# q turned by VectorE, attention in 32-row tiles: batches 1 to 7 of a linear-attention and expert kernel

## The chip, the cores and the metric

The kernel runs on one core of a Trainium2 chip. The time is that of the device for one execution, in microseconds (us). Five engines work side by side, each through its own list of instructions: TensorE (PE; its weight loads are listed as PEld), VectorE (DVE), ScalarE (ACT), GpSimd (POOL) and SyncE (SP), which starts most transfers. They wait for each other through semaphores. TensorE writes to PSUM[...]; ScalarE and VectorE carry results from there to SBUF.

## What is computed

The reference is linear attention, followed by a weighted sum of four experts. All is float32.

```python
# q, k, v: (8, 8, 576, 64) = batch, head, token, dimension
kv = np.einsum('bhsd,bhse->bhde', k, v)
out = np.einsum('bhsd,bhde->bhse', q, kv)
rms = np.sqrt(np.mean(out * out, axis=-1, keepdims=True) + 1e-06)
attn = out / rms * g_norm
# (B, H, S, D) -> (B*S, H*D): x is 4608 x 512
x = np.ascontiguousarray(attn.transpose(0, 2, 1, 3)).reshape(B * S, H * D)
p = domain_probs / (domain_probs.sum(-1, keepdims=True) + 1e-09)
for e in range(4):                       # w1: 4 x 512 x 1024, w2: 4 x 1024 x 512
    h = np.maximum(x @ w1[e], 0.0)
    out += p[:, e:e + 1] * (h @ w2[e])
```

## The kernel before

The work is cut into nine chunks of 512 tokens: the first 512 tokens of each of the eight batches, and a ninth that gathers the 64 left tokens of all batches. For each of four experts it goes through the nine chunks, with an up projection (`up`) and a down projection (`down`, `down_deep`). Both replace a product of 2x2 blocks by seven products of sums of blocks, most of them at two levels, so TensorE sees long rows of small products. They all go through one helper, which is why so much of the profile has line 356:

```python
    def halves_of(out_, lhsT, rhs, **kw):          # L352 to L356
        for half in range(2):
            cols = slice(half * D, (half + 1) * D)
            nc.tensor.matmul(out_[cols], lhsT=lhsT[:, cols], rhs=rhs, **kw)
```

Nothing is issued in the order of the source. Each operation is entered in a plan with a key (its place in the work), its buffers and a booked cost; `Plan.layout` then fixes the order of every engine before the launch. An engine takes the first operation that is ready within a reach beyond its oldest open one (`REACH`). PSUM banks come in four kinds of two banks each: u1 and u2 for the up products, db for the down products, ab for attention and others.

During the first expert, the attention of batch c + 1 runs inside the stage of chunk c. For batches 1 to 7 it works on pairs of heads (4 pairs), and on two groups of two pairs. Its steps, with the lines that the profile shows:

```python
        # 1. turn q (L693): per pair, four 128x128 transposes to one bank, a ScalarE copy to SBUF
                def turn(eng, bank=bank, qt=qt):
                    for r in range(NR):
                        rs = slice(r * P, (r + 1) * P)
                        if b:
                            nc.tensor.transpose(bank.ap[:, rs], qt.ap[:, rs], ident[:])
                            continue
                ...
        # 2. k.T @ v (L716) of the two pairs of a group, one bank, two 64-column halves (r: the head)
            def key_values(eng, bank=kbank, held=held):
                for o, (kt, vt) in enumerate(held):
                    sets = list(zip(kv_rows(kt), kv_rows(vt)))
                    for j, (ks, vs) in enumerate(sets):
                        for r in range(2):
                            nc.tensor.matmul(
                                bank.ap[r * D:(r + 1) * D, o * D:(o + 1) * D],
                                lhsT=ks[r], rhs=vs[r], start=(j == 0),
                                stop=(j == len(sets) - 1), skip_group_check=True,
                            )
        # 3. attend (L743): q @ kv in 64x64 tiles; head r contracts over its 64 rows, into bank raw[r]
            def attend(eng, raw=raw, kv=kv, pairs=pairs):
                for o, hp in enumerate(pairs):
                    for i in range(NR):
                        for c in range(2):
                            for r in range(2):
                                half = slice(r * D, (r + 1) * D)
                                at = i * P + c * D
                                nc.tensor.matmul(
                                    raw[r].ap[c * D:(c + 1) * D, (o * NR + i) * D:(o * NR + i + 1) * D],
                                    lhsT=qTs[hp].ap[half, at:at + D],
                                    rhs=kv.ap[half, o * D:(o + 1) * D],
                                )
        # 4. scaled(): squares (ScalarE, from PSUM), sums (VectorE), power (GpSimd),
        #    times 1/rms (VectorE, from PSUM) into x
        # 5. turn x (L761): per pair four transposes, then ScalarE copies with the gain
                def turn_x(eng, bank=bank, x=x, o=o):
                    for r in range(NR):
                        rs = slice(r * P, (r + 1) * P)
                        nc.tensor.transpose(
                            bank.ap[:, rs], x.ap[:, o * NT + r * P:o * NT + (r + 1) * P], ident[:])

        # 6. the 64 left tokens: turn q (L787), attend (L805), scale, turn x (L821), store to x_left
        def turn_rem(eng):
            for hp in range(NPAIR):
                nc.tensor.transpose(
                    tb.ap[:, hp * REM:(hp + 1) * REM], qr.ap[0:REM, hp * P:(hp + 1) * P],
                    ident[:REM, :REM],
                )
        ...
        def attend_rem(eng):
            for hp in range(NPAIR):
                for r in range(2):
                    half = slice(r * D, (r + 1) * D)
                    kv, o = kvs[hp]
                    nc.tensor.matmul(
                        rawr[r].ap[0:REM, hp * D:(hp + 1) * D],
                        lhsT=qTr.ap[half, hp * REM:(hp + 1) * REM],
                        rhs=kv.ap[half, o * D:(o + 1) * D],
                    )
        ...
        def turn_xrem(eng):
            for cc in range(NPAIR):
                nc.tensor.transpose(
                    xb.ap[:, cc * REM:(cc + 1) * REM], xr.ap[0:REM, cc * P:(cc + 1) * P],
                    ident[:REM, :REM],
                )
```

q is loaded for each head as `q[b, head, 0:512].rearrange("(p r) d -> p r d", r=4)` to columns that alternate between the two heads of a pair, in runs of 64 elements. The row order of x within a chunk, and so of the output, follows from this: partition p, block r is token 4p + r.

Batch 0 runs ahead of everything, with 128x512 up products (`up_plain`) in its wake; it has its own forms of steps 1 and 2.

## Time and profile before

| | before |
|---|---|
| time, median of three executions | 1688.22 us (1687.34 to 1689.27) |
| span of the profiled execution | 1685.7 us |
| instructions | 66495 |
| granted TensorE clock | 1.00 |
| DMA | 234.27 MB in 172330 packets, 61576 of them under 512 B |
| of attention, from 31 to 350 us: L693 / L716 / L743 / L761 | 100 / 480 / 768 / 96 records on PE |

In the page and the timeline, a row names the line, engine, operation, and output <- input by the names of the buffers with their numbers left out. A TensorE form like 128*64 is rows x columns of the tile of the array that is in use, followed by the moving operand's shape. A float32 matmul call leaves two records, a transpose one. Rows of a timeline give start, modelled length, engine, line, form and count; PE's lengths overlap, so the difference of two starts says more. Some of PE's records can be missing.

### The profile page before, as it was taken

The page shows a single profiled execution, that of the slowest core. Times are in us where ns is not written, and L with a number is a line of the kernel's source. Part 1 is how long each engine was busy: PE and PEld are TensorE (multiplying, and loading weights), DVE is VectorE, ACT ScalarE, POOL GpSimd, SP SyncE. Part 2 cuts the span into 40 slices and gives each one's busy share as a digit, 9 for nine tenths or more (in the row PEclk, how much of TensorE's full clock was granted, in tenths as well). Part 3 has the DMA queues.
Part 4 walks back from the last instruction along what each step waited for, and adds up shares of the span by engine and source line. Part 5 has one row for each costly group of instructions (what it writes and reads, how often), then busy time and mean ns, then how long its engine had stood idle before and what let it go on. Part 6 is the DMA issues. An engine that isn't in the chain of part 4 may idle for free.

```text
span 1685.7 us, 66495 instructions
## 1 busy us (share of the span) xinstructions
PE 1677.6 (100%) x29038; PEld 1572.0 (93%) x29038; DVE 1239.6 (74%) x2045; ACT 975.4 (58%) x2405; POOL 714.9 (42%) x672
## 2 busy tenths in 40 slices
PE   9999999999999999999999999999999999999998
PEld 6687888888889999999999999999999999999996
DVE  4865665575787788777787787877787886877774
ACT  3454555455455666566666566666666666666662
POOL 3613333333444344334455445444446446444431
PEclk9999999999999999999999999999999999999999
DMA  9955553642566344444568444445478444444442
GB/s 236 265 180 151 166 158 101 200 148 94 199 154 166 112 115 115 115 115 114 129 179 198 115 115 115 115 115 114 111 188 200 122 114 115 115 115 115 115 102 51
DMA packets 172330, 234.27 MB, mean 139 GB/s; under 512 B 61576, under 2 KB 112648, under 8 KB 172040
## 3 DMA queue, kind: packets, MB, share of 16 engines
q1 hardware_dynamic: 148968, 193.32, 36.7%
q0 software_dynamic: 23072, 36.71, 15.1%
q8 instruction: 228, 3.74, 0.9%
q14 instruction: 62, 0.51, 0.1%
HBM read 155.79 MB, written 74.19 MB: 136 GB/s over the span
## 4 chain that ended last, share of the span: by engine, by line
PE 98%; DMA 1%; SPq 0%; issue 0%; ACT 0%; DVE 0%
PE u L356 47%; PE db L356 32%; PE ab L356 14%; PE ab L716 1%; PE ab L761 1%; PE ab L693 1%; DMA small<-in_q_dram 1%; PE ab L743 1%; DMA xf<-x 0%; PE ab L805 0%; PE ab L787 0%; PE db L743 0%; PE ab L821 0%; PE ab L1440 0%; SPq L385 0%
## 5 line engine op out<-in xcount | busy, mean ns | idle before, releaser
L379 DVE TENSOR_TENSOR big<-big,big 128x1024 f32<-128x1024 f32 (+1 forms) x517 | 502.0, 985 | 43.3 <-ACT big L959 16.7
L356 PE MATMUL u<-xf,big 128*64 128x128 f32 x7072 | 505.0, 273 | 0.6 <-DMA xf<-x 0.6
L356 PEld LDWEIGHTS u<-xf,big 128*64 128x64 f32 x7072 | 409.4, 137 | 5.2 <-issue 0.9
L356 PE MATMUL u<-xf,w1y 128*64 128x128 f32 x5304 | 382.8, 273 | 0.0
L356 PE MATMUL db<-big,big 128*64 128x128 f32 (+1 forms) x4328 | 362.0, 307 | 0.0
L1003 DVE TENSOR_TENSOR big<-u,snap 128x256 f32<-128x256 f32 x464 | 194.0, 420 | 214.4 <-PE u L356 149.2
L356 PEld LDWEIGHTS u<-xf,w1y 128*64 128x64 f32 x5304 | 307.6, 137 | 4.5 <-issue 1.3
L356 PEld LDWEIGHTS db<-big,big 128*64 128x64 f32 x4328 | 264.4, 137 | 39.3 <-issue 0.5
L995 ACT ACTIVATE snap<-u 128x256 f32<-128x256 f32 x490 | 187.0, 382 | 194.5 <-PE u L356 140.6
L379 POOL TENSOR_TENSOR big<-big,big 128x256 f32<-128x256 f32 (+1 forms) x156 | 192.0, 1234 | 168.9 <-DVE big L379 75.0
L995 ACT ACTIVATE big<-u 128x256 f32<-128x256 f32 x464 | 176.7, 383 | 89.7 <-PE u L356 69.3
L379 POOL TENSOR_TENSOR big<-big 128x512 f32<-128x512 f32 (+1 forms) x76 | 95.3, 1255 | 161.4 <-DVE big L379 104.4
L1304 ACT ACTIVATE snap<-db 128x256 f32<-128x256 f32 (+1 forms) x230 | 82.1, 357 | 114.7 <-PE db L356 102.4
L959 ACT ACTIVATE big<-big 128x1024 f32<-128x1024 f32 x133 | 139.8, 1051 | 4.7 <-DVE big L379 4.3
L1161 POOL DMA_DIRECT2D out_dram<-big x98 | 88.4, 1025 | 56.0 <-ACT big L1138 43.6
L1312 DVE TENSOR_TENSOR big<-ab,snap 128x256 f32<-128x256 f32 x164 | 69.0, 421 | 58.2 <-PE ab L356 28.4
L1342 POOL TENSOR_TENSOR big<-big 128x512 f32<-128x512 f32 x34 | 44.0, 1296 | 154.1 <-DVE big L379 140.8
L995 ACT ACTIVATE u<-u 128x256 f32<-128x256 f32 x245 | 91.0, 372 | 28.6 <-PE u L356 14.1
L379 DVE TENSOR_TENSOR big<-big 128x512 f32<-128x512 f32 (+1 forms) x121 | 103.1, 855 | 0.5 <-ACT big L1138 0.2
L356 PE MATMUL ab<-big,big 128*64 128x128 f32 (+1 forms) x1352 | 94.7, 277 | 0.1
L356 PE MATMUL db<-small,big 128*64 128x128 f32 x1240 | 90.6, 273 | 0.0
L356 PE MATMUL ab<-kv,big 128*64 128x128 f32 x1200 | 83.2, 273 | 0.0
(178 smaller groups left out, 2412.4 us busy)
## 6 DMA issues: line engine op xcount, KB each, us to landing
xf<-x SPq DMA_DIRECT2D x108, 512.0 KB, 3.7
out_dram<-big POOLq DMA_DIRECT2D x82, 256.0 KB, 5.6
xf<-x_h SPq DMA_DIRECT2D x81, 256.0 KB, 3.5
xf<-x SPq DMA_DIRECT2D x81, 256.0 KB, 3.9
x<-xf SPq DMA_DIRECT2D x36, 512.0 KB, 4.9
big<-in_moe_w_dram SPq DMA_DIRECT2D x31, 512.0 KB, 5.2
x_h<-big SPq DMA_DIRECT2D x18, 512.0 KB, 3.4
big<-in_moe_w_dram POOLq DMA_DIRECT2D x17, 512.0 KB, 7.5
```

What stands on the lines that cost most here:

```text
L356: nc.tensor.matmul(out_[cols], lhsT=lhsT[:, cols], rhs=rhs, **kw)
L379: lambda eng: adder(eng).tensor_tensor(out=out_(), in0=a(), in1=b(), op=op),
L693: nc.tensor.transpose(bank.ap[:, rs], qt.ap[:, rs], ident[:])
L716: nc.tensor.matmul(bank.ap[r * D:(r + 1) * D, o * D:(o + 1) * D], lhsT=ks[r], rhs=vs[r], start=(j == 0), stop=(j == len(sets) - 1), skip_g ...
L743: nc.tensor.matmul(raw[r].ap[c * D:(c + 1) * D, (o * NR + i) * D:(o * NR + i + 1) * D], lhsT=qTs[hp].ap[half, at:at + D], rhs=kv.ap[half, ...
L959: lambda eng: nc.scalar.activation(out=b.ap[:], in_=b.ap[:], func=ACT.Relu),
L995: lambda eng: nc.scalar.activation(out=where(), in_=ps.ap[:, 0:HN], func=ACT.Copy),
L1003: lambda eng: nc.vector.tensor_tensor(out=block(whole, a, t), in0=src.ap[:, 0:HN], in1=add_.ap[:], op=ALU.add),
L1161: nc.gpsimd.dma_start(out=dst, in_=cell(i)[parts, :], accum_op=ALU.add)
L1304: lambda eng: nc.scalar.activation(out=where(), in_=group_of(ps.ap), func=ACT.Copy),
L1312: lambda eng: nc.vector.tensor_tensor(out=cell(tq, dq), in0=group_of(src.ap), in1=group_of(add_.ap), op=ALU.add,),
L1342: lambda eng: adder(eng).tensor_tensor(out=whole(to), in0=whole(a), in1=whole(b), op=ALU.add),
```

## The change

For batches 1 to 7 the change replaces `attention` (what it was stays as `opening`, for batch 0 alone).

- q: each group of four heads has one buffer of 128 x 1152, head a on partitions 32a to 32a + 31, sixteen tokens on each partition in runs of 4 KB, the left tokens behind them. VectorE turns it in place in 32x32 blocks, taking even and odd dimensions apart (`dh`). TensorE's turns of q and ScalarE's copies of them go.
- key-values: k is taken by the same parity, so each product has 32 columns; head a fills partitions 32a on.
- attend: the contraction runs over 32 rows, in tiles of 32 rows x 64 columns, one bank for each of four heads (two of kind ab, two of kind db), the two parities accumulated. The left tokens are a fifth block of the same group, so their own turn and attend go.
- the banks are copied to SBUF over the q buffer by VectorE or ScalarE, and the scaling works there.
- x turns: two pairs (eight transposes) in one operation; two 128x128 transposes for the left tokens.
- what follows from it: another order of the rows in output and probabilities for chunks 1 to 7, three small buffers in place of eight, and rules in the planner: operations marked `gang` may keep banks from others that would open them (`opens`), TensorE's reach goes from 0.7 to 1.1, and some down products get an order.

The core of the diff, with cuts marked:

```diff
-    REACH = {"PE": 0.7, "DVE": 0.9, "ACT": 0.9, "POOL": 0.9, "SP": 1.0}
+    REACH = {"PE": 1.1, "DVE": 0.9, "ACT": 0.9, "POOL": 0.9, "SP": 1.0}
...
+                        if op.gang and all(d.start is not None and d.end < t for d in op.deps):
+                            kept.update((b.kind, True) for b in op.outs if b.kind in BANKED)
...
+            plan.add(
+                when - 0.1, dve(QW),
+                lambda eng, qt=qt: nc.vector.transpose(out=by_parity(qt), in_=by_parity(qt)),
+                reads=[qt], writes=[qt],
+            )
...
+            def key_values(eng, bank=kbank, held=held):
+                sets = [list(zip(rows_of(kt), rows_of(vt))) for kt, vt in held]
+                last_ = len(sets[0]) - 1
+                for j in range(last_ + 1):
+                    for dh in range(2):
+                        for a in range(G):
+                            ks, vs = sets[a // 2][j]
+                            nc.tensor.matmul(
+                                bank.ap[a * R:(a + 1) * R, dh * D:(dh + 1) * D],
+                                lhsT=ks[a % 2][:, dh::2], rhs=vs[a % 2],
+                                start=(j == dh == 0), stop=(j == last_), skip_group_check=True,
+                            )
...
+            raw = [Buf(("ab", "ab", "db", "db")[a], f"raw{n}_{a}") for a in range(G)]
+
+            def attend(eng, raw=raw, kv=kv, qt=qt, s=s):
+                for t in range(NR + 1):
+                    for dh in range(2):
+                        for c in range(2) if t < NR else (s,):
+                            at_ = (2 * t + c) * P if t < NR else 2 * NT
+                            for a in range(G):
+                                rs = slice(a * R, (a + 1) * R)
+                                nc.tensor.matmul(
+                                    raw[a].ap[c * D:(c + 1) * D, t * D:(t + 1) * D],
+                                    lhsT=qt.ap[rs, at_ + dh:at_ + P:2],
+                                    rhs=kv.ap[rs, dh * D:(dh + 1) * D],
+                                    start=(dh == 0), stop=(dh == 1), skip_group_check=True,
+                                )
...
+            for a in range(G):
+                evacuate(
+                    when, raw[a],
+                    lambda a=a, raw=raw: raw[a].ap[:, 0:NR * D].rearrange("p (t e) -> p t e", e=D),
...
+            def turn_x(eng, turned=turned, qt=qt):
+                for o in range(2):
+                    for r in range(NR):
+                        nc.tensor.transpose(
+                            turned[o].ap[:, r * P:(r + 1) * P],
+                            qt.ap[:, o * NT + r * P:o * NT + (r + 1) * P], ident[:])
...
+        def turn_left(eng):
+            for o in range(2):
+                nc.tensor.transpose(
+                    xb.ap[:, o * P:(o + 1) * P], xr.ap[:, o * P:(o + 1) * P], ident[:])
...
+                return [(slice(0, P), whole.rearrange(
+                    "(p r a) d -> r a p d", r=NR, a=NR)[i])]
...
-                op.marks = ps, HN
+                    after=(second[-1:] if m in (1, 5) else []) + firsts[t:t + 1],
+                )
+                op.marks, op.opens = (ps, HN), m == 1
...
-                    after=(inner_last[-2:-1] or primed) if mm == 1 else seeds if mm == 5 else (),
+                    after=(inner_last[-2:-1] or primed) + (second[-1:] if mixed else []) if mm == 1 else seeds if mm == 5 else (),
```

## The prediction

> **What bounds the kernel now.** I read the page's first part, then the list of who waited for whom on TensorE, then the table by stretches of time, and last the timeline of TensorE. The first part says that PE has work nearly the whole span, while VectorE and ScalarE have slack:

> ```profile
> PE 1677.6 (100%) x29038; PEld 1572.0 (93%) x29038; DVE 1239.6 (74%) x2045; ACT 975.4 (58%) x2405; POOL 714.9 (42%) x672
> ```

> A busy PE alone could be a PE that is held up inside its pipeline. So the second view: everything that PE ever waited for, in the whole span.

> ```profile
> PE ab L1440 <- POOL ident masks.py:199: 1.4, 1, 1.4
> PE ab L697 <- DMA small<-in_q_dram: 1.0, 2, 0.6
> PE u L356 <- DMA xf<-x: 0.6, 1, 0.6
> PE ab L821 <- ACT big L769: 0.3, 1, 0.3
> ```

> 3.3 us in all, nearly all of it in the first 20 us. Time can come only from PE work that disappears. The third view shows what the other engines have to spare where attention runs. Columns: stretch, length, then busy us and (count) of PE, PEld, DVE, ACT, POOL, the granted clock, DMA share and GB/s.

> ```profile
> 31.00:75.00 44.00, 43.54 (x568) 23.63 (x566) 38.34 (x73) 19.31 (x47) 23.57 (x23) 1.00 0.93 246
> 75.00:120.00 45.00, 45.00 (x663) 36.10 (x659) 29.75 (x56) 24.05 (x56) 13.03 (x16) 1.00 0.66 211
> 120.00:180.00 60.00, 60.00 (x938) 48.79 (x938) 35.46 (x62) 30.05 (x70) 19.63 (x21) 1.00 0.47 138
> 180.00:240.00 60.00, 60.00 (x994) 50.73 (x990) 38.22 (x65) 32.29 (x75) 23.02 (x18) 1.00 0.50 149
> ```

> PE is full. From 120 us VectorE is busy 0.59 to 0.64 of the time, ScalarE 0.50 to 0.54. Only before 75 us is DMA near its limit.

> The fourth view gives the price of each piece of attention on PE. The printed length of a group is a modelled end; I use the difference between one start and the next.

> ```profile
> 86.33 0.61 PE L356 MATMUL u<-xf,big 128*64 128x128 f32 x8
> 86.76 0.61 PE L356 MATMUL u<-xf,w1y 128*64 128x128 f32 x8
> 87.30 0.66 PE L693 MATMUL ab<-ident,small 128*128 128x128 f32 x4
> 87.89 0.66 PE L356 MATMUL u<-xf,big 128*64 128x128 f32 x8
> 88.37 1.34 PE L716 MATMUL ab<-kv 120*64 120x64 f32 x40
> 89.54 1.04 PE L356 MATMUL u<-xf,big 128*64 128x128 f32 x16
> 90.52 0.46 PE L787 MATMUL ab<-ident,small 64*128 64x64 f32 x4
> 90.91 1.09 PE L356 MATMUL u<-xf,w1y 128*64 128x128 f32 x16
> ...
> 92.37 1.16 PE L743 MATMUL ab<-kv,small 64*64 64x64 f32 x64
> 93.46 0.66 PE L356 MATMUL u<-xf,w1y 128*64 128x128 f32 x8
> ...
> 103.16 0.68 PE L805 MATMUL ab<-kv,small 64*64 64x64 f32 x16
> 103.77 0.66 PE L356 MATMUL u<-small,big 128*64 128x128 f32 x8
> ```

> A group of eight 128*64 products between its like takes 0.43 us (86.33 to 86.76). Ahead of a group of another tile shape it takes 0.54 (86.76 to 87.30), after one 0.48 (87.89 to 88.37). Over all attention groups after 31 us I found medians of 0.10 and 0.05 us extra, so each **island** of attention in the stream of 128*64 products costs 0.16 us beside its own length.

> [...] The trace agrees for four tiles: 64 records of the 64*64 attend in 1.09 us are 17 ns apiece, while the median record lasts 218 ns. No run here yet shows eight. [...]

> **The change part by part, on PE, per batch (1 to 7).** Each Python matmul in float32 is two records here (32 calls, 64 records in L743), but a transpose is one.

> I count in **rounds**: calls divided by the tiles that work side by side. Attend: 32 calls on 4 tiles, 8 rounds, 1.09 us: 0.136 per round. Key-values: 20 calls on 2 column tiles, 10 rounds, 1.17: 0.117. Left tokens: 8 calls of which only two row tiles are at work, 4 rounds, 0.61: 0.152. The same price of some 0.12 to 0.15 us holds for all three, which is why I trust it for the new shapes.

> Before: q turns 4 x 0.585 = 2.34; turn of the left q 0.39; key-values 2 x 1.21 (mean of all its groups) = 2.42; attend 2 x 1.09 = 2.18; left attend 0.61; x turns 4 x 0.57 = 2.28; turn of the left x 0.41. Sum 10.6. As a check, all attention groups after 31 us add up to 75.6 us from start to start; 1.4 of these belong to batch 0, and 74.2 / 7 = 10.6. Islands: 80 in that stretch, 3 of batch 0, so 11 per batch, 11 x 0.16 = 1.75. Together **12.35 us per batch**.

> After:
> - the q turns, the turn of the left q and the left attend are gone: VectorE turns q, and the left tokens ride in the main attend.
> - key-values: 40 calls on 4 column tiles, 10 rounds as before: 2 x 1.21 = 2.42. It gains nothing; it makes the parity layout.
> - attend: per group 64 calls on 8 tiles are 8 rounds; the 8 calls for the left tokens use one column half, so 4 tiles, 2 rounds. 10 rounds x 0.136 = 1.36; twice, 2.72.
> - x turns: two pairs in one go, 8 transposes. The trace has eight in a row (83.20 to 84.23, four of x and four of q): 1.03. Twice, 2.06.
> - left x: 2 full transposes in place of 4 small ones, about 0.3 (half of 0.585).
> - islands: 2 + 2 + 2 + 1 = 7, x 0.16 = 1.1.

> Sum 8.6. Saved: 12.35 - 8.6 = 3.75 per batch, and 7 batches give **26 us**. The rest of PE's work (the nested seven-product up and down projections, 360 to 1686 us and most of what is before) keeps its instructions.

> **Beside PE.** Per batch the change takes from ScalarE the four q copies (0.6 each) and the left one (0.4), and adds, for whichever of VectorE and ScalarE is free, eight evacuations of 128x256 (0.38 to 0.42 by the rows of that shape) and eight small ones (I estimate 0.2), some 4.9 us; VectorE gets two turns of 1152 elements, which I estimate at 1.35 us each from the reduction of 1024 elements (1.215 us). Squares, reductions and the scaling stay about as long, but read SBUF. Net some 4 to 5 us per batch on two engines which in a stage of about 60 us have 20 to 30 us each to spare. That is hidden as a sum. The loads of q become 4 KB runs in place of 256 B runs, which can only relieve DMA in the first 75 us. The other output row order, four copies in the normalising of the probabilities and the scheduler's new rules are not PE work.

> **Rivals.** *A: the gang of four banks makes PE wait.* Attend needs both ab and both db banks at once; down products use db. Meanwhile only the up products are left, on u1 and u2, and these need a ScalarE or VectorE copy every 0.44 us. For it: the list of waits has ACT and DVE releasing banks just in time (L995 and L1003 lead their own lists because they wait for PE, so they run close behind it). Against it: the longer reach of PE's list and the rule that keeps banks closed to new openers are there to fill this time. 14 gangs x 0.3 us = 4 us is my allowance; at 1.5 us per gang the gain falls to some 5 us, time 1683. *B: issue bounds the eight tiles.* Should a record never follow another in under 17 ns, attend is 144 x 17 = 2.45 us instead of 1.36, key-values 80 x 17 = 1.36; loss 1.24 x 14 = 17 us, time 1679 (without A's allowance). For it: 17 ns is the closest the trace shows. Against: the price per round is the same at 2 tiles (29 ns a record) and at 4 (17 ns), so nothing has begun to saturate. *C: VectorE becomes the limit in the attention stages.* Its 0.6 share would rise to perhaps 0.67; I give that little weight, except before 75 us where it is at 0.87 and DMA at 0.93; there up to 3 us of batch 1's gain may be lost. *D: the work order improves by the new rules alone.* With 3.3 us of waits there is nothing to win.

> **Range and chances.** 1688.2 - 26 = 1662; plus 4 for A = 1666, and I take off nothing for D: **1666 us**. B with A's allowance is 1683, at the upper end; if the rounds are as short as key-values' 0.117 and no gang waits, attend is 0.19 us less on each of 14 groups, 2.7 us, and the x turns may be hidden next to each other with fewer islands: 1656. So 1655 to 1684. Faster by over 2% means under 1654.5: it would take a saving of 34 us where all of attention on PE is 86; 0.07. Slower by over 2% (above 1722) needs stalls of 60 us; 0.04. Within 2%: 0.89.

> **What would show it.** Right: the q turns gone from PE's groups for batches 1 to 7; attend groups of 144 records lasting 1.3 to 1.45 us from start to start; key-values of 80 records at about 1.2; PE's list of waits still under some 8 us; PE busy down by about 25 us with the rest of PE's groups unchanged in count. Wrong by A: waits of PE on u banks for DVE or ACT in the attention stages. Wrong by B: attend groups above 2 us. Wrong in total if PE's time outside attention changes, for example if the new order of projections makes more changes of tile shape.

## The result: 1.6% slower

The changed kernel takes **1715.85 us** (1710.64 to 1717.48), the kernel before 1688.43 beside it: ratio 1.0158, 95% interval 1.0135 to 1.018. The prediction was 1666 with a range of 1655 to 1684. It is outside, and the sign is wrong. That the time stayed within 2% of the old one, which the prediction gave 0.89, came true by luck: it was meant for a gain.

The first part of the page after:

```profile
PE 1674.4 (98%) x30452; PEld 1577.1 (92%) x30452; DVE 1268.0 (74%) x2065; ACT 973.2 (57%) x2419; POOL 762.8 (45%) x719
```

PE is busy 3 us less than before, not 26 less, and the span is 1713.6 us, so PE now stands idle for 39.2 us; before it was 8.1 (1685.7 - 1677.6). The list of who waited for whom on PE, longest first (us in total, times, longest), says for what:

```profile
PE u L371 <- DVE big L1236: 14.7, 9, 3.8
PE u L371 <- issue: 7.4, 4, 2.7
PE u L371 <- ACT u L1228: 2.7, 2, 2.2
...
PE ab L977 <- issue: 1.5, 2, 1.0
```

Two kinds of wait lead it. One is for VectorE's read of an up-product bank (L1236; a u bank comes free when it is read). The other is "issue": PE waits for nothing that the profile shows. The table by stretches (columns as in the prediction) says where. The changed kernel first, then the kernel before in a stretch far behind the attention:

```profile
75.00:120.00 45.00, 40.29 (x848) 33.54 (x846) 32.63 (x64) 22.14 (x57) 24.65 (x28) 1.00 0.75 236
120.00:180.00 60.00, 56.68 (x1146) 48.06 (x1144) 40.29 (x67) 29.21 (x69) 24.99 (x23) 0.97 0.50 160
...
700.00:1050.00 350.00, 344.67 (x6276) 343.86 (x6273) 267.12 (x428) 215.66 (x542) 162.60 (x149) 1.00 0.54 132
```

```profile
700.00:1050.00 350.00, 349.97 (x6408) 349.43 (x6406) 273.65 (x442) 219.69 (x552) 166.00 (x153) 1.00 0.54 133
```

From 700 to 1050 us no attention runs, only projections with the same instructions. Before, PE is idle for 0.03 us there; after, for 5.3, and 132 records fewer get done. So most of the loss is not where the change was thought to act. From 410 us to the end (the same table, summed) PE is idle for 24.4 us, before for 4.6; from 31 to 410 us it is 11.0 against 0.5. These are two losses with two causes.

**What VectorE waits for.** The timeline of all engines around one of the long waits (start, length, engine, line, what; in brackets the idle time before it and what ended it), cut to the chain:

```profile
469.95 1.90 PE L371 MATMUL db<-big,big 128*64 128x256 f32 x16
472.01 1.23 DVE L394 TENSOR_TENSOR big<-big,big 128x1024 f32<-128x1024 f32 x1 [4.92 <-DMA out_dram<-big]
473.16 0.42 DVE L1236 TENSOR_TENSOR big<-u,snap 128x256 f32<-128x256 f32 x1
...
473.63 0.55 PE L371 MATMUL u<-xf,w1y 128*64 128x128 f32 x6 [1.78 <-DVE big L1236]
```

Read it upwards. PE resumes when VectorE has read the u bank (L1236). VectorE stood still for 4.92 us until a transfer to the output had landed, because its next sum (L394) writes the buffer that this transfer was reading. So the chain is: an output lands late, its buffer comes free late, VectorE is late, PE waits. In the view of the output tensor, the waits of VectorE for it (us in total, times) are 40 us in the changed kernel:

```profile
DVE big L1236: 23.4, 8
DVE big L394: 16.7, 5
```

and 2 us in the kernel before:

```profile
DVE big L1003: 2.0, 2
```

The queues and the time from issue to landing are in the view of the DMA (queue: packets, MB, share; issues: KB each, median us to landing). Before:

```profile
q0 software_dynamic: 23072, 36.71, 15.1%
...
out_dram<-big POOLq DMA_DIRECT2D x82, 256.0 KB, 5.6
```

After:

```profile
q0 software_dynamic: 55328, 36.97, 15.8%
...
out_dram<-big POOLq DMA_DIRECT2D x92, 256.0 KB, 10.8
```

An accumulating transfer of 256 KB now lands after 10.8 us instead of 5.6. The planner books the buffer for 8 us. The queue carries 32,256 packets more: 84 transfers x 384, of 8 bytes each by the trace's records (0.26 MB in all).

**A wait can cost twice.** The granted clock of the whole span is 0.993, before 1.00. Around a wait at 866.95 to 870.75 us the table by stretches reads:

```profile
866.68:870.75 4.07, 0.28 (x6) 0.03 (x1) 1.61 (x3) 0.00 (x0) 0.21 (x1) 1.00 0.51 120
871.70:875.10 3.40, 3.40 (x38) 3.40 (x36) 3.40 (x3) 2.10 (x4) 3.10 (x3) 0.51 0.44 154
876.00:880.00 4.00, 4.00 (x78) 4.00 (x75) 3.25 (x5) 1.92 (x6) 1.71 (x2) 1.00 0.90 130
```

Soon after the wait PE works 3.4 us at half clock: 38 records in 3.40 us, and later 78 in 4.00 at full clock. There are six such windows of 3.41 us, and PE is busy in nearly all of them, so they cost about 6 x 1.7 = 10 us. In the kernel before there is none.

### The profile page after: what moved, and what is told of

The parts are those of the page before. It is cut to its first block, busy times and chain, and to the rows that moved or that the text cites. A ratio compares the mean times of both kernels' runs of the same rounds, so it can differ in the third digit from the quotient of the medians.

```text
span 1713.6 us, 69433 instructions
## 1 busy us (share of the span) xinstructions
PE 1674.4 (98%) x30452; PEld 1577.1 (92%) x30452; DVE 1268.0 (74%) x2065; ACT 973.2 (57%) x2419; POOL 762.8 (45%) x719
## 3 DMA queue, kind: packets, MB, share of 16 engines
q0 software_dynamic: 55328, 36.97, 15.8%
## 4 chain that ended last, share of the span: by engine, by line
PE 89%; DMA 7%; DVE 2%; issue 1%; POOL 1%; ACT 0%; SPq 0%; DVEq 0%; POOLq 0%; ACTq 0%
PE u L371 43%; PE db L371 28%; PE ab L371 13%; DMA out_dram<-big 5%; PE ab L977 1%; DVE big L394 1%; DMA xf<-x 1%; PE ab L1003 1%; PE ab L1035 1%; PE db L1003 1%; PE ab L1678 1%; DMA kv<-in_v_dram 0%; DVE big L1236 0%; POOL big L1580 0%; PE ab L712 0%
## 5 line engine op out<-in xcount | busy, mean ns | idle before, releaser
L394 DVE TENSOR_TENSOR big<-big,big 128x1024 f32<-128x1024 f32 (+1 forms) x505 | 493.4, 993 | 52.1 <-DMA out_dram<-big 16.7
L371 PE MATMUL u<-xf,big 128*64 128x128 f32 x7072 | 520.5, 274 | 4.5 <-issue 2.6
L371 PEld LDWEIGHTS u<-xf,big 128*64 128x64 f32 x7072 | 425.8, 138 | 9.5 <-issue 5.5
L371 PE MATMUL u<-xf,w1y 128*64 128x128 f32 x5304 | 395.8, 274 | 21.4 <-DVE big L1236 14.7
L371 PE MATMUL db<-big,big 128*64 128x128 f32 (+1 forms) x4408 | 371.9, 307 | 0.5 <-ACT snap L1542 0.5
L1236 DVE TENSOR_TENSOR big<-u,snap 128x256 f32<-128x256 f32 x452 | 189.8, 421 | 215.6 <-PE u L371 136.2
L371 PEld LDWEIGHTS u<-xf,w1y 128*64 128x64 f32 x5304 | 320.1, 138 | 27.8 <-DVE big L1236 17.2
L371 PEld LDWEIGHTS db<-big,big 128*64 128x64 f32 x4408 | 276.9, 137 | 38.4 <-issue 1.7
L394 POOL TENSOR_TENSOR big<-big,big 128x256 f32<-128x256 f32 (+1 forms) x170 | 187.6, 1109 | 151.4 <-DVE big L394 73.1
L394 POOL TENSOR_TENSOR big<-big 128x512 f32<-128x512 f32 (+1 forms) x77 | 100.9, 1312 | 152.3 <-DVE big L394 129.4
L1397 POOL DMA_DIRECT2D out_dram<-big x108 | 117.1, 1244 | 66.7 <-ACT big L1374 54.3
L394 DVE TENSOR_TENSOR big<-big 128x512 f32<-128x512 f32 (+1 forms) x128 | 113.7, 891 | 0.1
L371 PE MATMUL db<-small,big 128*64 128x128 f32 x1320 | 100.0, 273 | 0.0
L1374 ACT ACTIVATE big<-big,p_all 128x256 f32<-128x256 f32 x184 | 87.0, 502 | 1.6 <-POOL big L1580 1.0
## 6 DMA issues: line engine op xcount, KB each, us to landing
out_dram<-big POOLq DMA_DIRECT2D x92, 256.0 KB, 10.8
```

The costliest lines, as they stand in the source:

```text
L394: lambda eng: adder(eng).tensor_tensor(out=out_(), in0=a(), in1=b(), op=op),
L1236: lambda eng: nc.vector.tensor_tensor(out=block(whole, a, t), in0=src.ap[:, 0:HN], in1=add_.ap[:], op=ALU.add),
L1374: lambda eng: nc.scalar.activation(out=cell(i, half), in_=ap(), func=ACT.Copy, scale=prob()),
L1397: nc.gpsimd.dma_start(out=dst, in_=cell(i)[parts, :], accum_op=ALU.add)
```

## The experiments

Three theories. **Rows**: the new order of the output rows makes the accumulating transfers slow, and the rest follows. **Gang** (rival A of the prediction): the four banks of attend hold PE up. **Supply** (called C in the later expectations): PE's own instructions come too slowly where many short ones stand together. A letter in an expectation is explained there or ahead of it, where it stands for something else.

### e1: the change with the old output rows

Chunks 1 to 7 are sent in the old order. The rows of a chunk are thus permuted in the output; all bytes are written once.

```diff
-                return [(slice(0, P), whole.rearrange(
-                    "(p r a) d -> r a p d", r=NR, a=NR)[i])]
+                return [(slice(0, P), out[c * S:c * S + NT, :].rearrange(
+                    "(p r) d -> p r d", r=NR)[:, i, :])]
```

> The changed kernel with one thing put back: the output rows of chunks 1 to 7 are addressed as before (partition p, block r is row 4p + r), so the output's rows within a chunk are permuted; every engine's list stays the same. Theory A, the new row order slows the accumulating output transfers, accumulators come free late, VectorE and then TensorE wait: landing of these transfers falls from 10.8 to about 5.5 us, TensorE's waits after 410 us (some 16 us, and about 8 us of half clock after them) nearly vanish, time about 1692. Theory B, the new order of work (longer reach, gangs, extra dependencies) makes the waits: time stays at 1710 or more. Theory C, TensorE's own instruction supply in the attention stages is the main loss: time stays at 1708 or more, and the waits marked issue before 410 us stay.

Measured: 1686.98 us, ratio to before 0.9997 (0.9988 to 1.0006). The queue has 23,072 packets as in the kernel before, and the views show the landing and PE's stretch from 700 to 1050 us:

```profile
out_dram<-big POOLq DMA_DIRECT2D x92, 256.0 KB, 5.6
...
700.00:1050.00 350.00, 349.98 (x6411) 349.65 (x6409) 273.77 (x442) 219.17 (x552) 166.18 (x154) 1.00 0.54 133
```

No wait of PE for VectorE on a u bank is left, although the gang is untouched. Two half-clock windows remain, both after waits for issue (granted clock 0.92 from 75 to 120 us). One address pattern is worth 29 us by the medians, 27 by the ratios.

### e2: the kernel before with the new output rows

The reverse edit in the kernel before (rows permuted likewise), with its attention as it was.

```diff
-                return [(slice(0, P), out[c * S:c * S + NT, :].rearrange(
-                    "(p r) d -> p r d", r=NR)[:, i, :])]
...
+                return [(slice(0, P), whole.rearrange(
+                    "(p r a) d -> r a p d", r=NR, a=NR)[i])]
```

> The kernel before with only the new row addressing of the output for chunks 1 to 7 (rows permuted within a chunk; nothing else changed). Theory A: landing of the accumulating transfers goes from 5.6 to some 10 us, TensorE begins to wait for VectorE, time 1700 to 1715. Theories B and C: 1688, unchanged.

Measured: 1713.83 us, 1.0156 (1.0139 to 1.0173). The queue has 55,328 packets, and in the views of the DMA and of PE's waits stand:

```profile
out_dram<-big POOLq DMA_DIRECT2D x82, 256.0 KB, 10.7
...
PE u L356 <- DVE big L1003: 11.7, 7, 4.7
```

With e1 this settles it: the row order alone makes the loss, without the gang and without the new attention.

### e3: a row order that needs no second step

q is loaded so that token u x 32 + p stands on partition p (runs of 256 bytes in place of 4 KB). The rows of an output block are then consecutive. Everything is computed as in the reference.

```diff
-                    q[b, G * s + a, 0:NT, :].rearrange("(p u) d -> p (u d)", p=R), 128,
+                    q[b, G * s + a, 0:NT, :].rearrange("(u p) d -> p u d", p=R), 128,
...
-                    "(p r a) d -> r a p d", r=NR, a=NR)[i])]
+                return [(slice(0, P), whole.rearrange("(r p) d -> r p d", r=NR)[i])]
```

> The changed kernel computing the full reference with another order of tokens: q is loaded so that partition p of a head holds tokens 32u + p (runs of 256 B, as many packets as in the kernel before), block r of a chunk is rows 128r to 128r + 127, one plain run in the output; probabilities follow; booked costs and buffers unchanged. Theory A: landing 5.5 us or less, time about 1692, like the run with the old rows. Theories B and C: 1708 or more.

Measured: 1687.06 us, 0.9999 (0.9988 to 1.0011), landing 5.2 us. Its runs lie between 1681.87 and 1692.71 us. This is the change as it was meant, but for the long runs of q, and it is worth nothing. PE is busy for 1662.8 us, 14.8 less than before; but PE is idle for 20.8 us in place of 8.1, and 12.7 of the 14.8 are gone. PE's waits from 31 to 410 us:

```profile
PE u L371 <- issue: 5.0, 3, 3.0
PE ab L1030 <- DVE snap L873: 2.9, 1, 2.9
PE ab L972 <- issue: 1.4, 1, 1.4
PE db L998 <- issue: 1.3, 2, 0.8
```

7.7 us of issue and 2.9 for VectorE at the start of batch 1.

### e4: a longer booking

The planner is told that such a transfer takes 13 us, so that it reckons with the late buffer.

```diff
-                            op.end += 9.0 if op.kb == 512 else 8.0
+                            op.end += 9.0 if op.kb == 512 else 13.0
```

> The changed kernel with one number of its planner changed: an accumulating output transfer is booked as landing after 13 us in place of 8, so accumulators are planned to come free when they really do. Theory A in its narrow form (harm comes from a booking that is too short): waits for output transfers fall, time 1692 to 1705. If the lateness itself costs buffers: little gain, 1708 or more. Theories B and C: unchanged, about 1715.

Measured: 1701.72 us, 1.0081 (1.0066 to 1.0096). Waits for VectorE on u banks fall from 14.7 to 5.1 us. About half of the loss goes with the plan's wrong figure. The other half stays; that it is the lateness itself is the likely reading, and no run isolates it.

### e6: each send cut into four

The new row order stays, but each block of 128 rows goes as four transfers of 32 rows, each with one step.

```diff
-                return [(slice(0, P), whole.rearrange(
-                    "(p r a) d -> r a p d", r=NR, a=NR)[i])]
+                by_a = whole.rearrange("(p r a) d -> r a p d", r=NR, a=NR)[i]
+                return [(slice(32 * a, 32 * (a + 1)), by_a[a]) for a in range(NR)]
```

> The changed kernel with each output transfer of chunks 1 to 7 cut into four of 32 rows, one for each value of a, so that each has rows with one step only; same rows, same bytes, four times as many issues. If the two-step row pattern makes the extra small packets: the software queue falls from 55328 packets to about 23000; the four issues cost GpSimd some 3 us more per send, so time anywhere from 1690 to 1712. If the wider row step itself makes them: still 55000 packets and 1712 or more.

Measured: 1707.23 us, 1.0114 (1.0098 to 1.0129). A piece of 64 KB lands after 4.8 us, the last of a block's four 7.0 us after the first was issued (median, from the trace's records), and there is no packet of 8 bytes (27,104 packets in all; the 4,032 more than in the kernel before are of 4 bytes). So the same rows at the same distances land faster in one-step pieces (7.0 us for a block in place of 10.8), and VectorE no longer waits for a landing. But GpSimd now issues 356 times in place of 108 and is busy with it for 287 us in place of 117, and after 410 us PE still idles for 18 us. That the extra issues take back what was won is argued, not shown.

### e11 and e12: two steps of other lengths

The row step of e2 is varied in the kernel before: 16 by 8 rows (e11) and 2 by 64 (e12), in place of 4 by 32. Rows are permuted within their chunk. Theory K: how late a transfer lands and how many small packets it leaves goes with the number of steps in its slowest dimension. Theory P: any pattern of two row steps is slow in itself.

```diff
-                    "(p r a) d -> r a p d", r=NR, a=NR)[i])]
+                    "(p r a) d -> r a p d", r=NR, a=16)[i])]
```

> The kernel before with the two-step row order of the change in the output, but stepping 16 by 8 in place of 4 by 32 (a = 16; rows permuted within their chunk, all bytes written once). Two theories of why the 4 by 32 pattern landed in 10.7 us and left 8-byte packets. K: [...] Then here the landing is back at 5 to 6 us, the software queue has 23,072 packets as in the kernel before, and the time is 1687 to 1691 us. P: any two-step row pattern is slow in itself, by its small packets. Then the landing stays at 10 us or more, the queue keeps its 55,000 packets, and the time stays at 1707 us or more. I expect K.

> The same with a = 2: rows step 2 by 64. K: [...] at four it took 10.7 us, at sixteen 5.6, [...] I estimate 17 to 21 us. [...] there are 14 x 64 = 896 of them per transfer and about 98,000 packets in the software queue. Time: lateness grew by 5.1 us for 25 us lost, so some 10 us more could lose 50 more: 1740 to 1790 us. P: two long runs in place of four are a simpler pattern; landing at most 10.8 us, packets at most 55,000, time 1690 to 1714. I expect K.

Measured: e11 1687.83 us, 0.9998 (0.9989 to 1.0006); e12 1916.89 us, 1.135 (1.1327 to 1.1374). The DMA of e11:

```profile
q0 software_dynamic: 23072, 36.71, 15.2%
...
out_dram<-big POOLq DMA_DIRECT2D x82, 256.0 KB, 5.4
```

And of e12:

```profile
q0 software_dynamic: 98336, 37.31, 14.1%
...
out_dram<-big POOLq DMA_DIRECT2D x82, 256.0 KB, 17.2
```

A two-step pattern is not slow as such: with 16 outer steps it costs nothing and lands in 5.4 us (128 rows of one step: 5.6, in the kernel before), with 4 it lands in 10.7 us (e2), with 2 in 17.2. In these runs K holds in three ways. The landings grow as the dimension shrinks from 16 to 2: those of e11 and e2, put on a constant plus a share per step (3.6 + 28.3 / steps), give an estimate of 17.8 us for 2 steps. (The 5.6 in the expectation of e12 is that of the kernel before.) The packets of 8 bytes are 0, 384 and 896 per transfer; 896 was forecast, on an assumption of mine about where they come from that no run shows. And the data packets of 2 KB, each 178 ns in the median in all four kernels, overlap less (mean number in flight while any is, from the trace's records): 12.3 before, 12.7 in e11, 7.9 in e2, 5.1 in e12. Why fewer steps bring less overlap is not shown; the trace does not number the engines. The time of e12 is far above the 1740 to 1790 that I expected: PE is idle for 181 us and the granted clock is 0.954. The loss does not grow in proportion to the lateness: 5.1 us more to landing cost 26 us, 11.6 us more cost 229.

### e7, e8 and e5: the waits for issue

e7 (kernel before): attend is issued twice in batches 1 to 7, 128 records in a row, the second pass writing the same values.

```diff
-                for o, hp in enumerate(pairs):
+                for o, hp in list(enumerate(pairs)) * (2 if b else 1):
```

> The kernel before with each attend of batches 1 to 7 issued twice in a row (the same products into the same places; the result does not change). Pure work: 14 x 1.0 us more on TensorE, 1702. Theory C (a burst of some 256 instructions outruns the fetching of TensorE's instructions): waits marked issue appear in the attention stages, 3 us or more in all where the kernel before has less than 1, and the time is above 1705. Theory D (the waits of the changed kernel come from the extra work of VectorE and ScalarE or from its four held banks): no such waits, 1702.

Measured: 1704.62 us, 1.0097 (1.0082 to 1.0113). The pair takes 2.02 us in place of 1.09, so 14 more passes are 13 us of work, and 16 to 17 were added. Only one wait for issue (1.4 us) stands in the attention. So 128 records in a row at 16 ns don't outrun the supply; in this simple form the theory misses.

e8 (e3 without the odd dimensions): attend leaves out half of its products, 72 records in place of 144.

```diff
-                    for dh in range(2):
+                    for dh in range(1):
...
-                                    start=(dh == 0), stop=(dh == 1), skip_group_check=True,
+                                    start=True, stop=True, skip_group_check=True,
```

> The kernel of e3_q_order with the odd dimensions left out of attend (72 records in place of 144 per group, so the output lacks half of each sum over head dimensions); all other engines do the same work and the plan stays as it is. Pure work: attend falls from 1.7 to some 0.85 us, 14 x 0.85 = 12 us less, 1675. Theory C: the issue waits of the attention stages (some 8 us in e3_q_order) go as well, 1665 to 1669. Theory D: the waits stay, 1675.

Measured: 1668.19 us, 0.9879 (0.9865 to 0.9892), 19 us less than e3. Attend goes from 1.79 to 1.00 us, 14 x 0.79 = 11; most of the other 8 are the waits. PE's list from 31 to 410 us is now:

```profile
PE ab L1030 <- DVE snap L873: 2.9, 1, 2.9
...
PE u L371 <- issue: 0.3, 1, 0.3
```

Halving the records takes issue from 7.7 to 0.3 us. The wait for VectorE stays, as it should.

e5 (e3 with attend cut in two): 64 records, other work between, then 80.

```diff
+            first = plan.add(
+                at(2 * s + 1.0), {"PE": 0.7}, attend, reads=[qt, kv], writes=raw,
...
+                lambda eng, attend=attend: attend(eng, ts=range(2, NR + 1)),
+                reads=[qt, kv], parts=raw, after=[first, pause],
```

> The kernel of e3_q_order (full reference, contiguous output runs) with each attend cut in two pieces of 64 and 80 records, two other products of TensorE between them (a pause entered in the plan); the plan re-orders around it. Theory C (TensorE's list runs dry after the burst of 288 matmul and weight-load instructions in under 2 us, and this is what ate the saving of e3_q_order): waits marked issue before 410 us fall from about 8 us to under 3, the first piece of 64 records takes at most 0.65 us, time 1674 to 1682, though two more changes of tile shape per attend cost some 2 us in all. Theory D (the waits of the attention stages come from the extra work of VectorE and ScalarE or from banks being held): issue waits stay or turn into waits for VectorE, time 1685 or more.

Measured: 1689.53 us, 1.0006 (0.9998 to 1.0014). The pieces last 0.86 and 1.12 us, and from 31 to 410 us 5.9 us of issue waits stand (e3: 7.7), moved but not gone. A miss; it shows that the length of the row in itself is not what counts.

In the changed kernel 80 records of key-values and 144 of attend stand close together. The timeline of PE after the change shows one such place:

```profile
95.44 0.65 PE L371 MATMUL u<-xf,w1y 128*64 128x128 f32 x7
98.78 0.32 PE L371 MATMUL u<-xf,w1y 128*64 128x128 f32 x1 [2.69 <-issue]
```

PE stops inside one product, after seven of its eight records, where no bank or buffer can be at fault. The trace's instruction queue has a 16 KB packet landing at 97.46, and PE goes on 1.3 us later; after a packet at 133.12 it goes on at 134.54. The queue's packets before and after:

```profile
q8 instruction: 228, 3.74, 0.9%
```

```profile
q8 instruction: 239, 3.92, 1.0%
```

PE has 58,383 instructions in the trace before and 61,203 after, weight loads and waits included: one packet for every 256. From 31 us on, the traces of all runs together hold 50 waits for issue of over 0.15 us. Every one of them stands at the same place in a block of 256 (after 193 instructions beyond a multiple of 256), and every one ends 1.20 to 1.58 us after such a packet has landed. So these are waits for the next block of PE's instructions. What starts them is less clear. Most come in dense stretches: in the changed kernel 118 to 369 PE instructions started in the 4 us before each of its eight waits from 31 to 410 us, where the median stretch has 114 and the densest of the kernel before 234. But e7 goes through 326 and e3 through 399 without a wait, so no count of this kind separates the cases, and what decides when a packet is sent stays open. The one run that was to slow the pace without leaving products out, e5, did not slow it.

### e9 and e10: the useful half in the old tiles

e9 is the kernel before, with VectorE turning q, but laid out for the old 64x64 tiles: dimensions 0 to 31 and 32 to 63 of a head on 32 partitions each. Attend stays at 64 records, and the output rows are consecutive. e10 leaves batch 1 as it was in the kernel before. Both compute the whole reference.

```diff
+                        for h in range(2):
+                            at_ = 32 * (2 * r + h)
...
+                                q[b, 2 * hp + r, 0:NT, 32 * h:32 * (h + 1)].rearrange(
+                                    "(u p) d -> p u d", p=32), 64,
...
+                        lambda eng, qt=qt: nc.vector.transpose(out=qt.ap[:], in_=qt.ap[:]),
```

> The full reference from the kernel before with only one idea of the change: VectorE turns q, but in the layout that the old 64x64 attend needs (each head's dimensions 0 to 31 and 32 to 63 are loaded to two groups of 32 partitions, in runs of 128 B, so one 128x512 turn in 32x32 blocks gives what TensorE's four turns gave). Two banks for attend, key-values, left tokens and x turns as before; rows of the output in plain runs. TensorE loses 4 x 0.585 us of q turns and three to four islands (0.16 us each) per batch: 7 x 2.9 = 20 us. No burst of instructions is added. Expected by theories A and C: 1668 to 1674. If the planner's new order or the many small q packets before 75 us cost more: 1675 to 1685.

> The kernel of e9_turn_64 with batch 1 as in the kernel before (TensorE turns its q; its rows and probabilities as before); VectorE turns q for batches 2 to 7. In e9_turn_64 TensorE idled some 8 us between 31 and 75 us, waiting for VectorE's part of batch 1 while DMA was at 0.89, and lost 3.4 us more to a half clock after it. Theory A with C: these go, against 2.9 us of q turns that come back: 1679.7 - 11.4 + 2.9 = 1671. If the waits of the start are shifted and not removed: 1678 or more.

Measured: e9 1679.68 us, 0.994 (0.9927 to 0.9954), with 8 us of idle PE from 31 to 75 us. There PE waits 7.1 us for VectorE's scaling of batch 1 (L615); VectorE is busy for only 28.9 of the 44 us and itself waits, the longest time 4.7 us for the load of the probabilities, which this kernel splits. e10 **1672.93 us**, 0.9903 (0.9887 to 0.992), the fastest of all that do the whole work:

```profile
PE 1659.7 (99%) x28942; PEld 1562.4 (93%) x28942; DVE 1237.6 (74%) x2058; ACT 962.9 (58%) x2381; POOL 754.2 (45%) x683
```

PE is busy 17.9 us less than in the kernel before, with fewer instructions than before, and nearly all of that reaches the time (15.9 us).

## Why the prediction was wrong, step by step

- **The step that failed**: "The other output row order, four copies in the normalising of the probabilities and the scheduler's new rules are not PE work." True, and I took it to mean that it can't cost PE time. The row order doubled the landing of the transfers that free VectorE's buffers, from 5.6 to 10.8 us. e1 and e2 put its price at 29 and 26 us, nearly all of it beyond the attention. I had asked only what loads the change relieves (DMA's share from 31 to 75 us did fall, from 0.93 to 0.74), not what it does to the stores.
- **Attend, 1.36 us by rounds**: mis-sized. It takes 1.79 from start to start (median): 14 x 0.43 = 6 us. The price per round does not hold: the eight rounds on eight tiles take 1.41 us, 0.176 each, and the two of the left tokens 0.19 each. In the timeline after, the first 32 records go out at 9.3 ns apiece, about half of the 17 on four tiles, as eight side by side would have it; the next 96 take 11.6 ns each. Rival B, that records stop following each other closely enough, thus points the right way, with 12 ns on average in place of its 17; what sets the pace is not shown. These are the first records and the end of one group:

```profile
46.63 0.28 PE L1003 MATMUL ab<-kv,small 32*64 32x64 f32 x2
46.65 0.28 PE L1003 MATMUL db<-kv,small 32*64 32x64 f32 x2
...
48.23 0.23 PE L1003 MATMUL db<-kv,small 32*64 32x64 f32 x2
48.39 1.94 PE L371 MATMUL u<-big,big 128*64 128x512 f32 x8
```

- **The other pieces**: key-values 1.28 (1.21 predicted), x turns of eight 1.02 (1.03), left x 0.37 (0.3), islands 6.9 per batch (7). With attend at 1.79, the sum is 2 x 1.28 + 2 x 1.79 + 2 x 1.02 + 0.37 + 6.9 x 0.16 = 9.7 against 12.35, 19 us for seven batches. PE's busy time shows 14.8 (e3). Some 2 of the other 4 are groups of key-values and attend that run longer than the median without standing idle; the rest I did not place.
- **The allowance of 4 us for waits**: wrong in kind. The gang costs little: of waits on u banks for VectorE or ScalarE, the sign of rival A, 1.5 us stand from 31 to 410 us, in e1 0.5. In their place the changed kernel has 8.9 us of issue waits there, for the next block of instructions, which no rival named. Rival C's loss before 75 us does not come in the change itself (PE is busy for all 44 us from 31 to 75); in e3 PE waits 2.9 us for VectorE there.
- **"PE busy down by about 25, rest unchanged in count"**: the count is unchanged (26,800 records of the projections in both), and busy fell by 3, since six half-clock windows give 10 us back.

In sum, by the spans: 31 us more idle PE and 10 us at half clock, against 13 us of work saved, is +28 (1713.6 - 1685.7 = 27.9). Of the idle time some 20 us stand after 410 us and come from the rows; 10.5 stand from 31 to 410 us and belong to the attention itself.

## What to carry to other kernels

When a change reorders rows, look at the slowest dimension of the pattern that each store will have (16, 4 and 2 steps landed in 5.4, 10.7 and 17.2 us here), and at what its landing frees: an engine with 26% of slack (VectorE here) can still stop the bound one, if its buffer comes free late in a static plan. When work is packed into more and smaller tiles, price it by records as well as by rounds (0.176 us per round on eight tiles, 0.136 on four), and look for a version that keeps the record count down (e10 here). In a kernel whose bound engine never waits, the first waits can be worth more than their length: here 10 us at half clock came on top of 31 us more of idle PE.
